# A causal convolution followed by a routed mixture of experts: band built through DRAM, weights issued earlier, routing steps, outputs and the last slot placed anew

## The chip, the cores and the metric

The kernel runs on one core of one Trainium2 chip. The core has a matrix engine (TensorE, PE in the profile; its weight loads are shown as PEld), a vector engine (VectorE, DVE), a scalar engine (ScalarE, ACT), GpSimd (POOL) and a queue engine for transfers (SyncE, SP). Each engine works through its own instructions in order. Transfers are issued by SP, ScalarE or POOL and are moved by 16 DMA engines.

The metric is the device time of one execution in microseconds; lower is better. Times of several executions are given by their median. The profile is of one execution, whose own time stands beside it.

## What is computed

The reference, cut to what matters: x has shape (8, 3584, 192), there are 8 heads of 24 channels with 7 taps each, and 8 experts of width 1024.

```python
w = np.exp(weight - weight.max(-1, keepdims=True))
w = w / (w.sum(-1, keepdims=True) + 1e-09)               # softmax over 7 taps
out = np.einsum('hk,bskhg->bshg', w, x_unf)              # causal window of 7 rows
x = out.reshape(28672, 192)

logits = x @ w_gate                                      # 192 x 8
e_idx = np.argmax(logits, axis=1)
gate_w = probs[np.arange(N), e_idx]                      # softmax of the logits
eom = 1.0 / (1.0 + np.exp(-(x @ w_output_gate)))
for e in range(8):
    mask = e_idx == e
    h = np.maximum(x[mask] @ w1[e], 0.0)                 # 192 -> 1024
    out[mask] = gate_w[mask, None] * eom[mask, e, None] * (h @ w2[e])
```

## The kernel before

**Units.** The 28672 tokens are worked in 16 units of 1792 tokens, each of 16 blocks of 112. A unit passes three stages: front_a (convolution and router logits), front_b (routing: sorting its rows by expert into a stream in DRAM), and slots (the experts on 512 rows of one expert each).

**The constants ahead.** The taps (cw, L108) are loaded by SP, then the input of units 0 and 1 (load_x, L85 to L100, three transfers each for the first unit of a sequence, two otherwise). The taps' softmax is made by VectorE and ScalarE (L123 to L133). The convolution is a matmul against a band matrix per head, 118 input rows by 112 output rows. The band is filled by 14 predicated copies on VectorE (L142), each of which writes one tap of four heads along a diagonal, with a mask cut from an identity matrix (idp, L137). The router's weights wg come by eight small transfers on ScalarE's queue (L128, L129). The experts' weights stay resident in wres; they come in 32 pieces, four per expert, through POOL's queue. load_w(n) (L218) issues the next n of them.

**front_a(u)** (L298) is a generator with 16 steps. Eight steps are the convolution's matmuls, one head each (L303), with a copy out of PSUM into cv. Six steps are groups of four transposes (L317) with a copy into tt. One step is the router's matmul (L326) with the copy lt (L331), and the last is four transposes back (L335) and VectorE's copy gb (L340). After the convolution the input of unit u + 2 is requested (L309).

**evac** (L284) does the copies out of PSUM. It alternates between ScalarE and VectorE by the bit sync_flip, unless evac_on names an engine; while `fill` is not None, which is so ahead of the rounds, all go to ScalarE. In the rounds the front's PSUM tiles (pf) take turns in two banks.

**front_b(u)** (L347) has 12 steps. Step 1: the maximum, mask and exponent (L351 to L367, VectorE). Step 2: counts per expert (L374 on TensorE; nu, np, og and the gate gs on VectorE, L377 to L393). Step 3: prefix sums (L396 to L399 on TensorE, dm and pos on VectorE). Step 4: the first permutation masks and the destinations dd, dst, du (L431 to L446). Steps 5 to 12: for each pair of blocks four permutation matmuls (L457), a copy xs, and a scatter into the stream in DRAM (L475), which POOL issues from a list of pending ones (emit_in).

**Rounds.** After units 0, 1 and 2 have gone through both stages (L697 to L711), rounds follow for u = 2 to 15 (L742). A round has four slots (the last one eight full and three half ones, which bring their own copy of an expert's weights), and a slot has four positions, so a round has 16. At each position stand, in an order written out by hand: half of a slot's first layer at even positions (Slot.first, L626 and L633; ReLU on ScalarE, L646, for three quarters and on VectorE, L644, for the last), a quarter of the second layer of the slot before (second, L668), its copy y (L674) and output (L495, an indirect transfer issued by POOL, 128 rows each), steps of front_a(u + 2), steps of front_b(u + 1) (named fs) and of front_b(u + 2) (named fbn). The slots' input is read at position 7 for the round after (loads, L720).

Engines run in order, so the place of a step in this list is the place of its work on each engine. POOL's list holds scatters, outputs and weight issues. The transfers of SP and ScalarE share eight landing counters in the order of issue, and POOL has eight more; an issue waits until the transfer before it on its counter has landed.

Of the kernel before, what the change touches and what calls it, by code (L numbers as in the profile page):

```python
# [21 lines left out]
def kernel(  # L22
# [10 lines left out]
    nc = tc.nc  # L33
# [51 lines left out]
    def load_x(u):  # L85
# [8 lines left out]
        if u % UPB == 0:  # L94
# [14 lines left out]
                                    ap=[[0, 128], [KW, H], [1, KW]]))  # L109
    xts = {0: load_x(0)}  # L110
    xts[1] = load_x(1)


    ones_t = const.tile([128, 128], FP32)
    nc.vector.memset(ones_t, 1.0)
    identf = const.tile([128, 128], FP32)
    nc.gpsimd.affine_select(out=identf, in_=ones_t, pattern=[[-1, 128]],
                            compare_op=ALU.is_equal, fill=0.0, base=0,
                            channel_multiplier=1)
    band = const.tile([128, H, BT], FP32)  # L120
    nc.vector.memset(band, 0.0)
    cmx = const.tile([128, H], FP32)
# [3 lines left out]
    nc.scalar.activation(out=cw, in_=cw, func=AF.Exp)  # L126
    for i, (p0, p1, d0) in enumerate([(0, 128, 0), (0, 64, 128), (64, 128, 0), (0, 128, 64)]):
        nc.scalar.dma_start(wg[p0:p1, i, 0:E], moe_w_gate[d0:d0 + p1 - p0, :])  # L128
        nc.scalar.dma_start(wg[p0:p1, i, E:2 * E], moe_w_output_gate[d0:d0 + p1 - p0, :])  # L129
    csm = const.tile([128, H], FP32)  # L130
# [3 lines left out]
                            op=ALU.mult)  # L134

    idp = ps_f.tile([128, 512], FP32, tag="pf", name="idp")
    nc.vector.tensor_copy(out=idp[:, 0:128], in_=identf)  # L137
    idpu = idp.bitcast(U32)
    for h in (0, H // 2):
        for k in range(KW):  # L140
            m = idpu[:, k:k + BT]
            nc.vector.copy_predicated(  # L142
                out=band[:, h:h + H // 2, :],
                mask=m.unsqueeze(1).to_broadcast([128, H // 2, BT]),
                data=cw[:, h:h + H // 2, k:k + 1].to_broadcast([128, H // 2, BT]))
    ltri = const.tile([128, 128], FP16)
# [25 lines left out]
    idu = const.tile([128, NB], U32)  # L172
    nc.gpsimd.iota(idu, pattern=[[-BT, NB]], base=NOID, channel_multiplier=-1)
    idl = const.tile([128, NB], U32)
# [21 lines left out]
    nc.vector.tensor_copy(out=pos16, in_=poi.rearrange("p r j -> p (r j)"))  # L196

    wres = const.tile([128, E * WE], FP16)

    def w_pieces(e):
        o = e * WE
        w = moe_w1[e]
        return [
            (wres[:, o:o + F].rearrange("p (l c) -> p l c", l=2),
             bass.AP(tensor=w.tensor, offset=w.offset,
                     ap=[[F, 128], [64 * F + F // 2, 2], [1, F // 2]])),  # L210
            (wres[0:64, o + F:o + WA], w[0:64, F // 2:F]),
            (wres[64:128, o + F:o + WA], w[128:D, 0:F // 2]),
            (wres[:, o + WA:o + WE].rearrange("p (c d) -> p c d", d=D),
             moe_w2[e].rearrange("(c p) d -> p c d", p=128))]

    wq = deque(p for e in range(E) for p in w_pieces(e))

    def load_w(n):  # L218

        while n and wq:  # L220
            nc.gpsimd.dma_start(*wq.popleft())
            n -= 1

# [27 lines left out]
    for l in range(2):  # L251
# [7 lines left out]
        in0=o9, in1=s9, op=ALU.subtract)  # L259
    nc.vector.tensor_copy(out=lsum[:, c0 + 2 * NSEG:NK], in_=eqe[:, 0:E])  # L260


# [35 lines left out]
    def front_a(u, ahead=True):  # L298
# [31 lines left out]
        lt = pct.tile([128, 4 * BT], FP32, tag="lt", name="lt")  # L330
        evac(lt, pl[:, 0:4 * BT])  # L331
        yield
# [157 lines left out]

    def emit_out():

        while pout:
            y, oi, j = pout.popleft()
            i = nc.gpsimd.indirect_dma_start(  # L495
                out=out, out_offset=bass.IndirectOffsetOnAxis(ap=oi[:, j:j + 1], axis=0),
                in_=y[:, j, :], in_offset=None, bounds_check=N - 1, oob_is_err=False)
            nodep(i, "out", ("out",))
            last[0] = "out"
# [108 lines left out]
    class Slot:  # L608
        def __init__(self, xabi, w, inv):
            self.xa, self.xb, self.xi = xabi  # L610
            self.w, self.inv = w, inv
            self.n = self.xa.shape[1]
            self.nq = self.n // 128
            self.ht = []
# [34 lines left out]
        def second(self, q):  # L649
            if q >= self.nq:  # L650
                return
            if q == 0:
# [9 lines left out]
                                        op=ALU.bitwise_or)  # L662
            if q % 2 == 0:
                self.pp = ps_y.tile([128, 512], FP32, tag="py", name="pyt")
            o = (q % 2) * D
            for fc in range(FCH):
                w = WA + (fc // 2 + fc % 2 * (FCH // 2)) * D
                nc.tensor.matmul(self.pp[:, o:o + D],  # L668
                                 self.ht[fc // 2][:, fc % 2, q * 128:(q + 1) * 128],
                                 self.w[:, w:w + D],  # L670
                                 start=(fc == 0 and q % 2 == 0),
                                 stop=(fc == FCH - 1 and q % 2 == 1))
            if q % 2 == 1:
                nc.scalar.copy(out=self.y[:, q - 1:q + 1, :],  # L674
# [21 lines left out]

    load_w(8)  # L697
    drain(front_a(0))

    for u in range(U0 + 1):  # L700
# [3 lines left out]
        while drain(fb, 1):  # L704
            n += 1

            drain(fa, 1 if u == U0 or n > 8 else 2 if n < 8 else 0)
            emit_in(len(pend))
            if u < U0 and n > 4 and n % 2:
                load_w(1)  # L710
# [24 lines left out]
    fbn = front_b(U0 + 1)  # L735
    drain(fbn, 4)
    fill[0] = None

    prev = None
    for u in range(U0, NU):  # L742
        fs, fa, fbn = fbn, iter(()), iter(())
        if u + 2 < NU:
            fa, fbn = front_a(u + 2), front_b(u + 2)
        k = 0
        while k < len(todo):
            w, inv, xabi = todo[k]
            s = Slot(xabi, w, inv)
            for q in range(4):  # L750
                pos = 4 * k + q
                if 0 <= 16 * (u - U0) + pos - 4 < 16:
                    load_w(1)
                if q % 2 == 0:
                    s.first(q // 2)
                if pos in (0, 2, 4, 6, 8, 10, 12):
                    evac_on[0] = "act" if pos < 8 else None
                    drain(fa, 1)
                if pos == 14:
                    drain(fbn, 1)  # L760
                if prev is not None:
                    prev.second(q)
                    emit_out()
                if pos in (1, 3, 5, 7, 8, 9, 10, 11):
                    evac_on[0] = "dve" if pos < 8 else None
                    drain(fa, 2 if pos == 9 else 1)
                if pos < 8:
                    evac_on[0] = "act"
                    drain(fs, 1)
                    evac_on[0] = None  # L770
                    emit_in(len(pend))
                if pos == 12:
                    drain(fbn, 1)
                if pos == 15:
                    drain(fbn, 2)
                if pos == 7 and u + 1 < NU:
                    nxt = loads(u + 1)
# [65 lines left out]
```

## Time and profile before

| what | value |
|---|---|
| median of 9 runs | 624.03 us (622.06 to 626.73) |
| the profiled execution | 622.7 us |
| its span | 621.0 us |
| mean granted TensorE clock | 0.987 |
| first convolution starts | 11.17 us |
| first slot starts | 79.56 us |
| last output issued in the rounds | 613.11 us |
| POOL: outputs (L495) | 246, 996 ns each |
| POOL: scatters (L475) | 128, 1036 ns each |
| ScalarE: ReLU (L646) | 189, 1002 ns each |
| mean DMA rate | 142 GB/s, 88.12 MB |

In the profile a row of the timeline has the start in us, the duration in us, the engine, the line, the operation, the tiles (out<-in), and a count; in brackets is how long the engine had been idle before, and what ended that. A row of the groups has the busy time and the mean of one in ns, then the idle time before it with what ended most of it. The PEclk row gives the granted clock in tenths over 40 slices of the span. A row of the windows has the length, then for each engine the busy time and the number of instructions (PE, PEld, DVE, ACT, POOL), the granted clock, the share of the DMA engines and the GB/s.

### The profile page before, as it was taken

How to read it: one execution, taken by the hardware profiler on the slowest of the kernel's cores; microseconds unless marked ns; L12 is line 12 of the kernel's file. 1: busy time of each engine (PE TensorE's matmuls, PEld its weight loads, DVE VectorE, ACT ScalarE, POOL GpSimd, SP SyncE). 2: the span in 40 equal slices, each digit the busy share in tenths (PEclk: the TensorE clock that was granted, in tenths of full speed). 3: DMA queues.
4: the chain of work that ended last, by engine and by line, in shares of the span. 5: the costliest groups of instructions: out<-in, count | busy, mean ns of one | idle time of the engine just before them, and what ended most of it. 6: DMA issues, size and time to landing. Idle time of an engine off the chain costs nothing.

```text
span 621.0 us, 13578 instructions
## 1 busy us (share of the span) xinstructions
PE 574.3 (92%) x4544; PEld 358.5 (58%) x4544; DVE 380.8 (61%) x1310; ACT 382.4 (62%) x638; POOL 403.1 (65%) x419
## 2 busy tenths in 40 slices
PE   2999689999999999999999999999999999989992
PEld 1565337565566656656665666656566575646562
DVE  7678664765839477484856749476683947626231
ACT  1677556665666756665675666667566665657761
POOL 1377537787775757667575766757676675776674
PEclk9999979999999999999999999999999999999998
DMA  5999758993845455373555637255473425256631
GB/s 151 202 205 250 185 103 197 159 253 106 178 136 123 161 125 165 101 192 99 111 161 113 179 101 184 90 115 161 109 195 91 105 80 115 83 116 141 186 106 42
DMA packets 162567, 88.12 MB, mean 142 GB/s; under 512 B 116765, under 2 KB 153792, under 8 KB 162496
## 3 DMA queue, kind: packets, MB, share of 16 engines
q1 hardware_dynamic: 131872, 43.92, 31.5%
q0 software_dynamic: 29728, 43.30, 26.5%
q8 instruction: 36, 0.59, 0.4%
q14 instruction: 35, 0.29, 0.2%
q10 hardware_dynamic: 896, 0.03, 0.1%
HBM read 35.92 MB, written 43.06 MB: 127 GB/s over the span
## 4 chain that ended last, share of the span: by engine, by line
PE 78%; DVE 8%; ACT 5%; DMA 4%; issue 2%; POOL 1%; SPq 0%; ACTq 0%; POOLq 0%; DVEq 0%
PE pyt L668 21%; PE pp L626 18%; PE pf L303 11%; PE pp L633 10%; PE pf L457 7%; PE pf L317 5%; PE pf L326 4%; ACT ht L646 3%; DVE ht L644 2%; DVE band L142 1%; DMA xb<-xcg_sorted 1%; PE pf L335 1%; DMA out_dram<-y,oi 1%; ACT cv L291 1%; DMA xcg_sorted<-xs,du 1%
## 5 line engine op out<-in xcount | busy, mean ns | idle before, releaser
L495 POOL DMA_INDIRECT out_dram<-y,oi x246 | 244.9, 996 | 120.0 <-ACT y L674 54.4
L646 ACT ACTIVATE ht<-pp 128x1024 f16<-128x1024 f32 (+1 forms) x189 | 182.9, 1002 | 57.6 <-PE pp L633 56.7
L668 PE MATMUL pyt<-wres,ht 128*128 128x192 f16 x1920 | 190.4, 246 | 0.0
L475 POOL DMA_INDIRECT xcg_sorted<-xs,du x128 | 132.6, 1036 | 74.0 <-ACT xs L291 32.5
L668 PEld LDWEIGHTS <-ht 128*128 128x128 f16 x1968 | 166.5, 97 | 23.9 <-issue 10.4
L644 DVE TENSOR_SCALAR ht<-pp 128x1024 f16<-128x1024 f32 (+1 forms) x63 | 75.4, 1198 | 72.1 <-PE pp L626 72.1
L303 PE MATMUL pf<-xt,band 118*112 118x384 f32 x256 | 105.1, 504 | 11.7 <-DMA wg<-n_moe_w_output_gate_dram 11.2
L626 PE MATMUL pp<-xa,wres 128*128 128x512 f16 x240 | 93.0, 388 | 5.8 <-DMA xa<-xcg_sorted 5.8
L626 PE MATMUL pp<-xb,wres 128*128 128x512 f16 x240 | 91.3, 380 | 1.7 <-DMA xb<-xcg_sorted 1.7
L291 ACT CAST xs<-pf 128x388 f16<-128x388 f32 x128 | 61.8, 486 | 50.1 <-PE pf L457 48.4
L674 ACT COPY y<-pyt 128x384 f32<-128x384 f32 x123 | 58.5, 476 | 35.1 <-PE pyt L668 31.1
L626 PEld LDWEIGHTS <-wres 128*128 128x128 f16 x480 | 33.8, 97 | 67.7 <-issue 62.8
L633 PE MATMUL pp<-xa,wres 64*128 64x512 f16 x240 | 72.8, 383 | 0.0
L633 PE MATMUL pp<-xb,wres 64*128 64x512 f16 x240 | 72.8, 383 | 0.0
L457 PE MATMUL pf<-xrow,pm 112*128 112x194 f16 x512 | 64.5, 247 | 7.8 <-ACT cv L291 4.0
L457 PEld LDWEIGHTS <-pm 112*128 112x128 f16 x512 | 45.1, 98 | 35.1 <-issue 12.5
L427 DVE TENSOR_SCALAR pm<-pos,pos 112x256 f16<-112x256 f16 x256 | 62.8, 310 | 0.0
L422 DVE TENSOR_TENSOR xrow<-cv,gs 112x384 f16<-112x384 f32 x121 | 62.0, 551 | 0.0
L303 PEld LDWEIGHTS pf<-xt,band 118*112 118x112 f32 x256 | 41.5, 182 | 27.2 <-DVE band L142 12.1
L293 DVE COPY cv<-pf 112x384 f32<-112x384 f32 x48 | 26.5, 552 | 43.4 <-PE pf L303 43.3
L291 ACT COPY cv<-pf 112x384 f32<-112x384 f32 x80 | 38.1, 479 | 21.6 <-PE pf L303 21.2
L317 PE MATMUL pf<-identf,cv 112*128 112x112 f32 x384 | 49.3, 259 | 0.7 <-ACT cv L291 0.7
(135 smaller groups left out, 432.7 us busy)
## 6 DMA issues: line engine op xcount, KB each, us to landing
xt<-in_x_dram SPq DMA_DIRECT2D x8, 1344.0 KB
xt<-in_x_dram SPq DMA_DIRECT2D x8, 1260.0 KB
out_dram<-y,oi POOLq DMA_INDIRECT x246
wres<-in_moe_w_dram POOLq DMA_DIRECT2D x8, 384.0 KB
wd<-wres SPq DMA_DIRECT2D x3, 768.0 KB
wres<-in_moe_w_dram POOLq DMA_DIRECT2D x8, 256.0 KB
xcg_sorted<-xs,du POOLq DMA_INDIRECT x128
xcg_sorted<-zrow SPq DMA_DIRECT2D x8, 256.0 KB
```

The source lines that it names most:

```text
L291: nc.scalar.copy(out=o, in_=i)
L303: nc.tensor.matmul(pc[0:BT, 0:NB * GH], band[0:KI, h, :], xt[0:KI, :, h * GH:(h + 1) * GH], start=True, stop=True)
L317: nc.tensor.matmul(pt[:, j * BT:(j + 1) * BT], cvf[0:BT, m * 2 * D + i * 128:m * 2 * D + (i + 1) * 128], identf[0:BT, 0:BT], is_transpose= ...
L427: nc.vector.tensor_scalar(out=pms[i][P, l, :], in0=pos16[P], scalar1=pos[P, l * NG + i:l * NG + i + 1], scalar2=None, op0=ALU.is_equal)
L457: nc.tensor.matmul(ps[:, r * XW:(r + 1) * XW], pm[P, l, r * 128:(r + 1) * 128], xr[P, l * NG + i, :], start=(r == 0 and l == 0), stop=(r = ...
L475: i = nc.gpsimd.indirect_dma_start(out=xcg2, out_offset=bass.IndirectOffsetOnAxis(ap=du[:, i:i + 1], axis=0), in_=xs.rearrange("p r w -> p ...
L495: i = nc.gpsimd.indirect_dma_start(out=out, out_offset=bass.IndirectOffsetOnAxis(ap=oi[:, j:j + 1], axis=0), in_=y[:, j, :], in_offset=Non ...
L626: nc.tensor.matmul(pps[r][:, l, :], w[:, o2:o2 + 128], x, start=(r == 0), stop=(r == 1))
L633: nc.tensor.matmul(pps[r][:, l, :], w[p0:p0 + 64, c:c + 128], x[p0:p0 + 64], start=(r == 1), stop=(r == 0))
L644: nc.vector.tensor_relu(out=ht, in_=pps[r])
L646: nc.scalar.activation(out=ht, in_=pps[r], func=AF.Relu)
L668: nc.tensor.matmul(self.pp[:, o:o + D], self.ht[fc // 2][:, fc % 2, q * 128:(q + 1) * 128], self.w[:, w:w + D], start=(fc == 0 and q % 2 = ...
```

## The change

- **wg** comes on SP's queue, between the inputs of units 0 and 1, instead of on ScalarE's.
- **The band.** Only heads 0 and 1 are filled by predicated copies (seven of 2 x 112). For heads 2 to 7 ScalarE copies the taps into a row of zeros, one line of 229 per head; the lines go to DRAM, and a second transfer reads the band from them, each partition one element further along. This gives the rows of a block in reverse order, so the mask comes from an anti-diagonal matrix (antif), and the row numbers (idu) count the other way.
- **Weights.** Twelve pieces are issued right after the constants, ahead of zrow and front_a(0), instead of eight after them; four more in the opening's loop for unit 0 alone, instead of four each for units 0 and 1. The other sixteen go at positions 8 to 23 of the rounds instead of 4 to 19.
- **front_a(0).** The copies of its six transposes alternate between ScalarE and VectorE; ahead of the rounds the copy lt is split in two halves, one per engine.
- **First round.** One step of unit 3's front_b is done ahead of the first slot instead of four; the others stand in the round, at positions 0 to 10, with two at position 2.
- **Order in a round.** Steps of front_a ahead of the second layer stand at positions 0, 2, 4, 6, 8, 9, 10 instead of 0, 2, ..., 12; those of fbn at 12, 13 (after it) and 14, 15 (before it) instead of 12 (after), 14 (before) and two at 15 (after).
- **Round 14** keeps up to eight outputs in the list during its first eight positions.
- **The last slot** has its own PSUM tile, copy and output for each 128 rows.

```diff
@@ -108,41 +108,56 @@
     xts = {0: load_x(0)}
+    for i, (p0, p1, d0) in enumerate([(0, 128, 0), (0, 64, 128), (64, 128, 0), (0, 128, 64)]):
+        nc.sync.dma_start(wg[p0:p1, i, 0:E], moe_w_gate[d0:d0 + p1 - p0, :])
+        nc.sync.dma_start(wg[p0:p1, i, E:2 * E], moe_w_output_gate[d0:d0 + p1 - p0, :])
     xts[1] = load_x(1)
...
+    antif = const.tile([128, 128], FP32)
+    nc.gpsimd.affine_select(out=antif, in_=ones_t, pattern=[[1, 128]],
+                            compare_op=ALU.is_equal, fill=0.0, base=-127,
+                            channel_multiplier=1)
...
+    HB = 2
+    LW = BT + KI - 1
     band = const.tile([128, H, BT], FP32)
-    nc.vector.memset(band, 0.0)
+    nc.vector.memset(band[:, 0:HB, :], 0.0)
+    wline = const.tile([1, H - HB, LW], FP32)
+    nc.vector.memset(wline, 0.0)
+    wldr = nc.dram_tensor("tap_lines", (H - HB, LW), FP32, kind="Internal").ap()
...
-    for i, (p0, p1, d0) in enumerate([(0, 128, 0), (0, 64, 128), (64, 128, 0), (0, 128, 64)]):
-        nc.scalar.dma_start(wg[p0:p1, i, 0:E], moe_w_gate[d0:d0 + p1 - p0, :])
-        nc.scalar.dma_start(wg[p0:p1, i, E:2 * E], moe_w_output_gate[d0:d0 + p1 - p0, :])
...
+    nc.scalar.copy(out=wline[:, :, BT - 1:KI], in_=cw[0:1, HB:H, :])
+    nc.scalar.dma_start(wldr, wline)
+    nc.scalar.dma_start(band[0:KI, HB:H, :],
+                        bass.AP(tensor=wldr.tensor, offset=wldr.offset,
+                                ap=[[1, KI], [LW, H - HB], [1, BT]]))
     idp = ps_f.tile([128, 512], FP32, tag="pf", name="idp")
-    nc.vector.tensor_copy(out=idp[:, 0:128], in_=identf)
+    nc.vector.tensor_copy(out=idp[:, 0:128], in_=antif)
     idpu = idp.bitcast(U32)
-    for h in (0, H // 2):
-        for k in range(KW):
-            m = idpu[:, k:k + BT]
...
+    for k in range(KW):
+        m = idpu[:, 128 - BT - k:128 - k]
+        nc.vector.copy_predicated(
+            out=band[:, 0:HB, :],
+            mask=m.unsqueeze(1).to_broadcast([128, HB, BT]),
+            data=cw[:, 0:HB, k:k + 1].to_broadcast([128, HB, BT]))
...
-    nc.gpsimd.iota(idu, pattern=[[-BT, NB]], base=NOID, channel_multiplier=-1)
+    nc.gpsimd.iota(idu, pattern=[[-BT, NB]], base=NOID - (BT - 1), channel_multiplier=1)
...
+    load_w(12)
...
-        evac(lt, pl[:, 0:4 * BT])
+        if fill[0] is None:
+            evac(lt, pl[:, 0:4 * BT])
+        else:
+            nc.scalar.copy(out=lt[:, 0:2 * BT], in_=pl[:, 0:2 * BT])
+            nc.vector.tensor_copy(out=lt[:, 2 * BT:4 * BT], in_=pl[:, 2 * BT:4 * BT])
...
-    def emit_out():
-        while pout:
+    def emit_out(keep=0):
+        while len(pout) > keep:
...
-            if q % 2 == 0:
+            if q % 2 == 0 or self.end:
                 self.pp = ps_y.tile([128, 512], FP32, tag="py", name="pyt")
...
-            if q % 2 == 1:
+            if self.end:
+                nc.scalar.copy(out=self.y[:, q, :], in_=self.pp[:, 0:D])
+                pout.append((self.y, self.oi, q))
+            elif q % 2 == 1:
...
-    load_w(8)
-    drain(front_a(0))
+    fa = front_a(0)
+    drain(fa, H)
+    for i in range(6):
+        evac_on[0] = "dve" if i % 2 else "act"
+        drain(fa, 1)
+    evac_on[0] = None
+    drain(fa)
...
-            if u < U0 and n > 4 and n % 2:
+            if u == 0 and n > 4 and n % 2:
                 load_w(1)
...
     fbn = front_b(U0 + 1)
-    drain(fbn, 4)
+    drain(fbn, 1)
     fill[0] = None
...
+        last_s = 10 if u == U0 else 7
...
-                if 0 <= 16 * (u - U0) + pos - 4 < 16:
+                if 0 <= 16 * (u - U0) + pos - 8 < 16:
                     load_w(1)
                 if q % 2 == 0:
                     s.first(q // 2)
-                if pos in (0, 2, 4, 6, 8, 10, 12):
-                    evac_on[0] = "act" if pos < 8 else None
+                evac_on[0] = "act" if pos < 8 else None
+                if pos in (0, 2, 4, 6, 8, 9, 10):
                     drain(fa, 1)
-                if pos == 14:
+                if u == U0 and pos == 2:
+                    drain(fs, 1)
+                if pos in (14, 15):
                     drain(fbn, 1)
                 if prev is not None:
                     prev.second(q)
-                    emit_out()
+                    emit_out(8 if u == NU - 2 and pos < 8 else 0)
+                evac_on[0] = "dve" if pos < 8 else None
                 if pos in (1, 3, 5, 7, 8, 9, 10, 11):
-                    evac_on[0] = "dve" if pos < 8 else None
                     drain(fa, 2 if pos == 9 else 1)
-                if pos < 8:
+                if pos <= last_s and not (u == U0 and pos == 2):
                     evac_on[0] = "act"
                     drain(fs, 1)
-                    evac_on[0] = None
                     emit_in(len(pend))
-                if pos == 12:
+                evac_on[0] = None
+                if pos in (12, 13):
                     drain(fbn, 1)
-                if pos == 15:
-                    drain(fbn, 2)
-                if pos == 7 and u + 1 < NU:
+                if pos == last_s and u + 1 < NU:
                     nxt = loads(u + 1)
```

## The prediction

> **What bounds the kernel now.** I read the page's engine rows first, then its groups, then the timeline of three stretches: the opening, a round in the middle, the end.
>
> ```profile
> PE 574.3 (92%) x4544; PEld 358.5 (58%) x4544; DVE 380.8 (61%) x1310; ACT 382.4 (62%) x638; POOL 403.1 (65%) x419
> PEclk9999979999999999999999999999999999999998
> ...
> L457 PE MATMUL pf<-xrow,pm 112*128 112x194 f16 x512 | 64.5, 247 | 7.8 <-ACT cv L291 4.0
> ```
>
> TensorE is busy for 92% of the span, so in the middle only its waits can be won. From round 3 to round 13 a round's first matmul follows the last one's by 36.67 us (timeline), and each round holds two waits over 0.12 us:
>
> ```profile
> 482.46 1.23 DVE L644 TENSOR_SCALAR ht<-pp 128x1024 f16<-128x1024 f32 x1 [0.44 <-PE pp L626]
> ...
> 484.40 0.23 PE L398 MATMUL pf<-lsum,np 64*128 64x128 f16 x1 [0.31 <-DVE og L384]
> ```
>
> L398 needs np, which VectorE makes only after this 1.23 us ReLU. The second is L457's, 0.40 us in that round: ScalarE empties the conv's PSUM bank late. The opening has other limits:
>
> ```profile
> 0.82 3.76 DMA cw<-in_weight_dram
> ...
> 11.17 4.37 PE L303 MATMUL pf<-xt,band 118*112 118x384 f32 x8 [11.17 <-DMA wg<-n_moe_w_output_gate_dram]
> 15.87 2.83 PE L303 MATMUL pf<-xt,band 118*112 118x384 f32 x8 [0.33 <-DVE band L142]
> ...
> 24.61 2.10 PE L303 MATMUL pf<-xt,band 118*112 118x384 f32 x6
> ...
> 72.73 0.98 POOL L475 DMA_INDIRECT xcg_sorted<-xs,du  x1 [1.90 <-DMA xcg_sorted<-xs,du]
> 74.02 0.98 POOL L475 DMA_INDIRECT xcg_sorted<-xs,du  x1 [0.30 <-DVE dl L353]
> ...
> 79.56 0.59 PE L626 MATMUL pp<-xa,wres 128*128 128x512 f16 x1 [3.44 <-DMA xa<-xcg_sorted]
> ```
>
> conv(0) waits for x(0) (11 us; the releaser named is a neighbour on the same counters) and half way for the band. conv(1) starts at 24.61 when unit 0's last transposes leave TensorE. The first slot starts at 79.56, behind the last scatter at 74.02. The end belongs to POOL:
>
> ```profile
> 545.50 0.98 POOL L475 DMA_INDIRECT xcg_sorted<-xs,du  x1 [0.30 <-ACT ht L646]
> ...
> 575.78 0.98 POOL L495 DMA_INDIRECT out_dram<-y,oi  x1 [3.55 <-ACT y L674]
> ...
> 613.11 0.99 POOL L495 DMA_INDIRECT out_dram<-y,oi  x1 [0.30 <-DMA out_dram<-y,oi]
> ```
>
> From 575.78 on POOL issues an output every 1.287 us without a gap.
>
> **The change, part by part.** The sum goes against the profiled 622.7 (span 621.0 and 1.7 around it); the median, 624.03, is 1.33 above that, which I add at the end.
>
> *1. Band and conv(0): 0.* Fourteen copies of 448 (9.49 us for x14) become seven of half the width; by half the duration 7 x 0.33 = 2.3 us, so VectorE runs 7.1 us ahead, and heads 0 and 1 are ready at 8.7, before x(0). Heads 2 to 7 go tap copy, DMA to DRAM, DMA back. The only row for a small load's whole way is cw, 3.76: 6.4 + 3.76 + 3.76 = 13.9, with issue about 14.4. The slower row is wg's (issued 5.53, landed 11.12: 5.6 us), which gives 17.6. I take 14.4, as cw moves on an empty queue as this does, though x(0) is in flight beside it. Then conv(0) ends at 18.3 instead of 18.55 (bounds -0.7 and +1.8), and with the two copy engines and the halved lt copy gb is ready some 0.4 earlier. That gain is lost in the next term.
>
> The Trainium skill ("DMA: Bandwidth & Descriptors", section "Anatomy of one DMA") gives a fixed cost of about 2.0 us for one DMA, and this trace shows 3.76 for 28 KB. By the page the band would be there at 10.4 and x(0) alone would set conv(0); by the row it is four us later. The row decides, and the sum would be 0 by either.
>
> *2. Unit 1's input: +3.4.* The load of x(1), issued at 11.14 before, now stands on SP behind the eight wg loads. SP and ScalarE share the landing counters in their order of issue, so wg's last load waits for the band's landing; x(1) is issued at about 14.6. Beside it POOL now issues twelve weight pieces as soon as VectorE has made eqe (18.52 - 7.1 = 11.4): data from about 15.2 (first issue 19.07 to first data 3.2 us in the trace). x(1) is 1.45 MB. Alone, at the 206 GB/s that the windows show for 11 to 18 us, it lands at 14.6 + 1 + 7.0 = 22.6 and nothing is late. With weights beside it:
>
> ```profile
> 22.00:33.00 11.00, 9.91 (x58) 5.65 (x52) 7.33 (x30) 6.36 (x17) 2.70 (x5) 1.00 1.29 228
> ```
>
> Half of 228 GB/s is 12.7 us: x(1) at 28.4, conv(1) 3.8 later. There the software and the hardware queue did move equal shares (1.46 and 1.45 MB in 18 to 33), so I take the half. 0.4 of it was won before: +3.4. Bounds: 0, and +7.4 if the band lands at 17.6 (x(1) issued 18.5, landed 32.3).
>
> *3. POOL before the first slot: -3.1.* Four weight issues in unit 1's phase go. The last xs of unit 2 is ready at 69.2, yet the last scatter is issued at 74.02, since scatters queue 1.29 us apart behind weights and 1.90 us for a counter. By xs alone it would be 70.9: -3.1. Bounds 0 and -4. First slot: 79.56 + 3.4 - 3.1, about 79.9. Only one step instead of four of unit 3 stands ahead of it: 0, TensorE waits there anyway; the cover is the 3.44 us of the row, and without it the steps would cost 3 us.
>
> *4. The clock at the first slot: 0.*
>
> ```profile
> 79.50:90.00 10.50, 9.78 (x36) 3.97 (x37) 5.12 (x19) 5.38 (x8) 1.96 (x2) 0.69 0.50 97
> ```
>
> 0.69 granted is half clock for 62% of 10.5 us, a loss of 3.25. The wait ahead of it shrinks from 7 to about 4 us and loses its few matmuls. It may keep the clock (-3.25) or not (0); a new wait of 4 us for x(1) may itself cost up to 3.25. Nearest is the row itself, so 0.
>
> The Trainium skill ("TensorE: Matmul & The Clock Gate", section "What's actually happening") says that an idle window of about 3.4 us halves the clock and a busy one of that length restores it. That speaks against the change, since part 2 makes a second wait above that length. By the rule the sum would be up to 3.3 higher than by the row.
>
> *5. Steps of unit 3 moved into the first round: +0.45.* L374 and L396 to L399 now stand between slots; beside the wait they took 482.36 to 482.51 and about 0.30 more.
>
> *6. Rounds: -3.4.* The counts step moves two positions forward and the prefix step one. L374 then comes 1.52 us before L396, with no ReLU in front of nu and np (0.9 us): L398's wait goes (3.5 of its 4.1 us lie in rounds). The moved prefix also leaves L457 the bank that is not ScalarE's: it then needs dd 2.63 us after the group, TensorE arrives after 2.83, so its wait goes too (4.0 and 0.40 for dd): -7.9. In their place: the transposes of group 2 directly follow group 1. A round has 23 alternating copies, so in every other round ScalarE has group 0's copy, behind
>
> ```profile
> 468.79 1.94 ACT L646 ACTIVATE ht<-pp 128x1024 f16<-128x1024 f32 x2 [0.34 <-PE pp L633]
> ...
> 470.61 0.54 ACT L291 COPY tt<-pf 128x448 f32<-128x448 f32 x1
> ```
>
> and ends at 471.15, where the bank is wanted at 470.66: 0.49. L335 then follows the lt copy with 0.09 (ScalarE) or 0.18 us (VectorE) missing: 0.75 per two rounds, six times, +4.5. Net -3.4; bounds -7.9 (VectorE takes the copies) and 0 (the waits only change place). Two points make the net fragile: the 0.2 us of slack at L457, and which engine the alternation hits. Weights later in the rounds (positions 8 to 23): 0, covered by some 9 us before a slot of that expert; without cover a piece late by one position costs 2.3 us.
>
> *7. The end: -0.6.* Outputs held back let the last scatter of round 14 go at 537.9 instead of 545.50, which removes waits of 2.04 and 0.66 us at 551. But POOL then has 58 outputs from 539.1 on: the last at 539.1 + 57 x 1.287 = 612.5, against 613.11. The 3.55 us gap is all that it can close, and most of that is taken by the outputs held. The split last slot: 0, as its y is ready 2.3 us before POOL gets to it. If POOL had the room, 2.7 could come.
>
> Sum: 0 + 3.4 - 3.1 + 0 + 0.45 - 3.4 - 0.6 = -3.25. 622.7 - 3.25 + 1.33 = 620.8. Own range 618.5 to 623.
>
> **The rivals.** *B, the opening gains too, 616.5.* x(1) in time (-3.4: 617.4) or the clock kept at the first slot (617.5), both 614.1. For it: x(1) lands at 22.6 if the hardware queue keeps its 206 GB/s. Against: the equal shares.
> *C, slower, 628.* x(1), queued behind the chain of tap line and band, lands at 32.3 (+4.0 over my term) and TensorE, idle for 8 us, returns at half clock (+3.25): 620.8 + 7.25. It is slower than before from a start of conv(1) at about 30.3 with the clock closed, 33.5 without. For it: 5.6 us of the wg row; against: cw's 3.76.
> *D, the waits in the rounds change place only, 624.2* (620.8 + 3.4). For it: ScalarE's queue at 468.79 stands before group 0's copy in any round; against: L398's cause, the ReLU, is really gone.
>
> **How the numbers follow.** A 0.42, B 0.22, C 0.20, D 0.16. A measurement of this kernel tells about 0.3% (1.9 us) from no change: faster is below 622.2, slower above 625.9. Faster: 0.33 of A, all of B, 0.02 of D: 0.57. Slower: 0.17 of C, 0.04 of D: 0.21. The rest, 0.22, is the same. The range 614 to 627 takes in B down to both gains and C up to a start of conv(1) near 31; about 0.15 is left out.
>
> **What would show it.** In the new profile: conv(1) at 28.4 with a wait for x(1) over 3 us (C: past 30.3; B: under 25). The last scatter before the first slot within 2 us of the last xs. L398 with waits under 0.1 in the rounds and none on cv at L457; new waits at L317 in every other round of about 0.5 and L335 of 0.1 to 0.2; first-to-first about 36.4. No wait at 551 for xa, POOL without a gap from there, and the last output issued within 1 us of 612.5 - 2.6. I am wrong if conv(1) keeps its start, if a round gains over 0.6 us or loses, or if POOL has gaps after 550.

## The result, and the profile after

The change makes the kernel slower: 647.29 us (median of 10 runs, 645.03 to 649.6) against 623.84 us before (31 runs), a ratio of 1.0375 with a 95% interval of 1.0354 to 1.0397. The forecast was 620.8 with a range to 627, so sign and range were wrong. The profiled execution has a span of 644.1 us against 621.0.

The starts of the slots' first matmuls (L626 before, L647 after) part the 23.1 us by stage:

| stage | before, us | after, us | difference |
|---|---|---|---|
| start to first slot | 79.56 | 102.23 | +22.67 |
| round u = 2 | 37.35 | 43.06 | +5.71 |
| rounds 3 and 4 | 74.34 | 74.67 | +0.33 |
| rounds 5 to 13 | 330.06 | 325.55 | -4.51 |
| round 14 | 29.90 | 26.81 | -3.09 |
| round 15 to the end | 69.79 | 71.78 | +1.99 |

So nearly all of it is lost ahead of the first slot, and a quarter of that again in the first round; the later rounds do gain. The page of the changed kernel, engine rows and slices first, then a DMA queue, then two groups:

```profile
PE 578.0 (90%) x4544; PEld 358.8 (56%) x4544; DVE 379.0 (59%) x1312; ACT 378.6 (59%) x635; POOL 408.4 (63%) x420
...
PE   1079986989999999999999999999999999999991
...
q10 hardware_dynamic: 712, 0.32, 0.2%
...
L320 PE MATMUL pf<-xt,band 118*112 118x384 f32 x256 | 106.4, 510 | 33.4 <-DMA band<-tap_lines 21.3
...
L478 PE MATMUL pf<-xrow,pm 112*128 112x194 f16 x512 | 64.7, 247 | 5.9 <-DVE pm L448 4.4
```

TensorE's second slice is empty (a slice is 16 us), and the convolution's idle time is now the band's transfer, 21.3 us, which was not there before. q10 carries the tap lines and the band: 712 packets for 0.32 MB. L478 (L457 before) no longer waits for cv.

The chain of what ended last, in the opening (start, duration, what):

```profile
0.82 3.52 DMA cw<-in_weight_dram
...
6.13 5.97 DMA tap_lines<-wline
...
12.13 23.31 DMA band<-tap_lines
...
35.48 4.76 PE pf L320 x8
```

The taps go out in 5.97 us and come back as a band in 23.31. The timeline of SP shows what else hangs on that landing:

```profile
12.63 0.58 SPq L112 DMA_DIRECT2D wg<-in_moe_w_gate_dram  x1
35.46 0.33 SPq L113 DMA_DIRECT2D wg<-n_moe_w_output_gate_dram  x1
35.84 0.43 SPq L98 DMA_DIRECT2D xt<-in_x_dram  x1
```

wg's last load shares the band's landing counter and stands until 35.46, with unit 1's input behind it. conv(1) starts at 47.30, 22.69 later than before, which is the whole delay of the first slot.

The end of the first round, from TensorE's timeline:

```profile
145.29 0.59 PE L647 MATMUL pp<-xa,wres 128*128 128x512 f16 x1 [3.06 <-DMA xa<-xcg_sorted]
146.09 0.58 PE L647 MATMUL pp<-xb,wres 128*128 128x512 f16 x1 [0.22 <-DMA xb<-xcg_sorted]
```

TensorE waits for the second round's slots, which had no such wait before. The waits of TensorE between 182 and 545 us (total, times, longest):

```profile
PE pf L334 <- ACT tt L308: 1.7, 5, 0.3
```

The two waits of each round before, for og and for cv, are gone; in every other round there is the transposes' wait.

### The profile page after: what moved, and what is told of

It is laid out like the page before. It is cut to its first block, busy times and chain, and to the rows that moved or that the text cites. A ratio compares the mean times of both kernels' runs of the same rounds, so it can differ in the third digit from the quotient of the medians.

```text
span 644.1 us, 13571 instructions
## 1 busy us (share of the span) xinstructions
PE 578.0 (90%) x4544; PEld 358.8 (56%) x4544; DVE 379.0 (59%) x1312; ACT 378.6 (59%) x635; POOL 408.4 (63%) x420
## 3 DMA queue, kind: packets, MB, share of 16 engines
HBM read 36.24 MB, written 43.06 MB: 123 GB/s over the span
## 4 chain that ended last, share of the span: by engine, by line
PE 79%; DMA 10%; DVE 4%; ACT 3%; issue 2%; POOL 1%; SPq 0%; POOLq 0%; ACTq 0%; DVEq 0%
PE pyt L689 23%; PE pp L647 17%; PE pf L320 12%; PE pp L654 10%; PE pf L478 6%; PE pf L334 5%; PE pf L343 4%; DMA band<-tap_lines 4%; DMA xb<-xcg_sorted 2%; ACT ht L667 2%; DMA out_dram<-y,oi 2%; PE pf L356 1%; DMA xcg_sorted<-xs,du 1%; DMA tap_lines<-wline 1%; POOL out_dram L516 1%
## 5 line engine op out<-in xcount | busy, mean ns | idle before, releaser
L516 POOL DMA_INDIRECT out_dram<-y,oi x246 | 248.1, 1009 | 114.7 <-ACT y L698 47.7
L496 POOL DMA_INDIRECT xcg_sorted<-xs,du x128 | 135.0, 1054 | 100.2 <-ACT xs L308 67.9
L320 PE MATMUL pf<-xt,band 118*112 118x384 f32 x256 | 106.4, 510 | 33.4 <-DMA band<-tap_lines 21.3
L647 PE MATMUL pp<-xa,wres 128*128 128x512 f16 x240 | 93.3, 389 | 8.2 <-DMA xa<-xcg_sorted 7.9
L647 PE MATMUL pp<-xb,wres 128*128 128x512 f16 x240 | 91.8, 382 | 1.1 <-DMA xb<-xcg_sorted 1.1
L320 PEld LDWEIGHTS pf<-xt,band 118*112 118x112 f32 x256 | 42.2, 185 | 50.4 <-DMA band<-tap_lines 22.4
L478 PE MATMUL pf<-xrow,pm 112*128 112x194 f16 x512 | 64.7, 247 | 5.9 <-DVE pm L448 4.4
L647 PEld LDWEIGHTS <-wres 128*128 128x128 f16 x480 | 34.8, 98 | 60.7 <-issue 60.3
L448 DVE TENSOR_SCALAR pm<-pos,pos 112x256 f16<-112x256 f16 x256 | 64.6, 321 | 0.0
L478 PEld LDWEIGHTS <-pm 112*128 112x128 f16 x512 | 44.4, 97 | 30.9 <-issue 13.7
```

The costliest lines, as they stand in the source:

```text
L320: nc.tensor.matmul(pc[0:BT, 0:NB * GH], band[0:KI, h, :], xt[0:KI, :, h * GH:(h + 1) * GH], start=True, stop=True)
L448: nc.vector.tensor_scalar(out=pms[i][P, l, :], in0=pos16[P], scalar1=pos[P, l * NG + i:l * NG + i + 1], scalar2=None, op0=ALU.is_equal)
L478: nc.tensor.matmul(ps[:, r * XW:(r + 1) * XW], pm[P, l, r * 128:(r + 1) * 128], xr[P, l * NG + i, :], start=(r == 0 and l == 0), stop=(r = ...
L496: i = nc.gpsimd.indirect_dma_start(out=xcg2, out_offset=bass.IndirectOffsetOnAxis(ap=du[:, i:i + 1], axis=0), in_=xs.rearrange("p r w -> p ...
L516: i = nc.gpsimd.indirect_dma_start(out=out, out_offset=bass.IndirectOffsetOnAxis(ap=oi[:, j:j + 1], axis=0), in_=y[:, j, :], in_offset=Non ...
L647: nc.tensor.matmul(pps[r][:, l, :], w[:, o2:o2 + 128], x, start=(r == 0), stop=(r == 1))
```

## The experiments

Each kernel was compared with runs of the kernel before on the same chip, so the ratios are what to compare. In the expectations the rounds are counted from the first as 0: "rounds 3 to 11" are u = 5 to 13. The start of conv(1) in the changed kernel that the first one gives as 49.8 is that of a later group; it is 47.30.

### Why the band's read takes 23 us

**Two transfers for the band, 112 and 6 rows.**

```diff
-    nc.scalar.dma_start(band[0:KI, HB:H, :], ...)
+    for r0, r1 in ((0, BT), (BT, KI)):
+        nc.scalar.dma_start(band[r0:r1, HB:H, :], ...offset + r0...)
```

> The changed kernel, but the band's read from the tap lines is two transfers, rows 0 to 111 and rows 112 to 117, instead of one of 118 rows. Three theories of why the read took 23.3 us (issued 12.13, landed 35.48). S (spread): a transfer of 118 rows falls on few of the 16 DMA engines; early in it, 95 packets of 34 ns came per us, the work of about 3 engines. Then the band lands before 18 us, conv(1) starts near 30 instead of 49.8, and the time falls by 17 to 20 to 627 to 630. W (weights): the twelve early weight pieces crowd out any read beside them. Then the split changes nothing: landing after 30, time 645 to 649. N (narrow rows): reading 448-byte rows one element apart is slow however it is cut. Then the landing is after 30 as well, time 645 to 649.

Measured: 636.65 us, ratio 1.0180 (1.0127 to 1.0232). The band is there at 15.6 us, with 397 packets in the fullest microsecond instead of 95. S, that the read is spread over few engines, is right about the landing. The time fell by about 11 us and not by 17 to 20, for two reasons that TensorE's timeline shows:

```profile
11.58 2.87 PE L321 MATMUL pf<-xt,band 118*112 118x384 f32 x4 [11.58 <-DVE pe L225]
15.90 7.23 PE L321 MATMUL pf<-xt,band 118*112 118x384 f32 x12 [1.45 <-DMA band<-tap_lines]
...
34.16 4.15 PE L321 MATMUL pf<-xt,band 118*112 118x384 f32 x6 [5.10 <-DMA xt<-in_x_dram]
```

After the pause of 1.45 us the twelve matmuls take 0.60 us each; in the kernel before the second eight took 0.35 each. conv(0) ends at 23.0 instead of 18.6. And conv(1) waits 5.10 us for its input and then takes 4.15 us for six matmuls instead of 2.10. The window of these six has the reason (the three figures at its end are the granted clock, the share of 16 DMA engines, and GB/s):

```profile
34.10:38.30 4.20, 4.14 (x7) 1.74 (x8) 0.00 (x0) 1.17 (x3) 0.00 (x0) 0.50 1.16 262
```

TensorE comes out of this wait at half clock.

**The weights held until the band has landed.** GpSimd first copies one element of the band's last head.

```diff
+    bseen = const.tile([1, 1], FP32)
+    nc.gpsimd.tensor_copy(out=bseen, in_=band[0:1, H - 1, 0:1])
     load_w(12)
```

> The changed kernel, but GpSimd first reads one element of the band from DRAM, so that the twelve weight pieces are issued after the band's landing. The read has the DMA engines almost to itself. S: 708 packets at the 95 per us seen early in it take 7.5 us, landing at 20.5 to 22, time about 634 to 637. W: landing before 17, time about 627 to 630. N: like S or later.

Measured: 637.43 us, ratio 1.0213 (1.0174 to 1.0252); the second part of conv(0) starts at 22.47 after 8.12 us of waiting. The landing (22.4) and the time lie just beyond what S named, and far from W's: without the weights the read is still slow, 10 us from its issue, and with them it takes 23. So both count. The window in which nothing but the band moves:

```profile
15.00:20.00 5.00, 0.00 (x0) 0.00 (x0) 0.00 (x0) 0.00 (x0) 0.00 (x0) 1.00 0.15 40
```

0.15 of 16 engines is 2.4. Where all are at work the same figure is about 1.1 per engine (1.09 between 16 and 17 us before, as x loads), so about two of sixteen move the band.

**One transfer of 128 rows.** The lines are ten zeros longer, and ten more rows are read that nothing uses.

```diff
-    LW = BT + KI - 1
+    LW = BT + 127
-    nc.scalar.dma_start(band[0:KI, HB:H, :], ... [[1, KI], ...
+    nc.scalar.dma_start(band[0:128, HB:H, :], ... [[1, 128], ...
```

> The changed kernel with the band read in one transfer, of 128 rows instead of 118 (the lines in DRAM ten zeros longer, ten more rows that nothing reads). It parts two readings of the split's gain. Row count: a count that 16 divides (128, like 112) spreads over all DMA engines; then one transfer lands as early as the split did, 15 to 17, more than 250 packets in its fullest us, time 634 to 639. Rival, number of transfers: each transfer gets few engines, and two got more than one; then the landing stays after 28 and the time at 645 to 649.

Measured: 636.98 us, ratio 1.0226 (1.0196 to 1.0255). The band lands in time for 16.00, as with the split, and 415 packets come in the fullest microsecond. Its window:

```profile
14.00:15.00 1.00, 0.55 (x1) 0.00 (x0) 0.00 (x0) 0.41 (x1) 1.00 (x3) 1.00 0.94 190
```

0.94 instead of 0.15, and some 185 of the 190 KB in this window are the band's (415 packets, nearly all of 448 bytes). The packets also count the engines: beside the band's 708 packets of 448 bytes the trace of the changed kernel has 2 packets of 4 bytes at the end of the read, that of the split 22, and that of this run, beside 768, 16. One closing packet for each engine that takes part would be 2, 16 + 6 and 16. It is the count of rows, not of transfers.

**Unit 1's input ahead of wg,** in the kernel with the split.

```diff
     xts = {0: load_x(0)}
+    xts[1] = load_x(1)
     for i, (p0, p1, d0) in enumerate(...):      # wg
...
-    xts[1] = load_x(1)
```

> The run with the split read of the band (e1_split), with the input of unit 1 issued on SP ahead of the eight wg loads again. In e1 conv(1) waited 5.1 us for it and its first six matmuls then took 4.15 us instead of 2.10. Theory (x(1) is late because it stands behind wg's last loads, which wait for the band's landing, and then shares the DMA engines with the weights): the wait goes, conv(1) starts within 1 us after unit 0's last transposes, the first slot comes 5 to 8 us earlier (84 to 87), time 629 to 632. Rival: x(1) then runs beside x(0) and the tap line and makes the band land later; first slot after 89, time above 634.

Measured: 637.09 us, ratio 1.0201 (1.0169 to 1.0234), the first slot at 90.80 instead of 91.51. The rival is right. conv(1) follows at once (35.79 after transposes from 35.09), so the wait was indeed that of the order on SP. But the tap line and the band then move beside x(1): the band's last part comes at 23.1 instead of 15.6, and the delay has only changed its place.

In all four of these runs the first slot starts between 90.80 and 91.55 and conv(1) between 33.90 and 35.79, though the band is there at 15.6, 16.0, 22.4 or 23.1. So the two engines and the weights beside them make about half of the 22.7 us. The other 11 us stay as long as the band, wg and x(1) hang on one another and x(1) or the band shares the DMA engines with other loads; these two causes were not parted.

### The rest of the change without the band

**VectorE's band in the changed kernel.** Fourteen predicated copies again, with the reversed mask; no tap lines.

> The changed kernel with the whole band made by VectorE again (14 predicated copies of four heads), no tap lines; all other parts as changed. If the read of the band is the cause of the 22.67 us by which the first slot came later (102.23 against 79.56), the first slot is back at 77 to 81 and the time at 621 to 626: the rounds' gain of 4.5 in rounds 3 to 11 against a first round that is 5.7 longer. If the twelve early weight pieces, wg on SP's queue or the missing routing steps are the cause, the first slot stays above 85 and the time above 630.

Measured: 626.46 us, ratio 1.0032 (1.0002 to 1.0061), half a microsecond above what was expected; the first slot is at 80.39. Without the band's transfer 21.8 of the 22.7 us are gone. One more thing changes with it: GpSimd's weights wait for eqe, which VectorE now makes behind the fourteen copies, and are issued from 19.82 instead of 12.39. That this is not the cause is shown by the run with the weights held: there they are issued from 22.61, and the first slot is at 91.55. But the first round takes 45.14 us and the second 39.40, which the rounds' gain does not pay. TensorE's row at the second round's first slot, and the window of that slot:

```profile
125.53 0.59 PE L638 MATMUL pp<-xa,wres 128*128 128x512 f16 x1 [2.81 <-DMA xa<-xcg_sorted]
```

```profile
125.50:138.60 13.10, 12.58 (x72) 7.35 (x73) 6.68 (x26) 6.43 (x10) 8.76 (x10) 0.75 1.17 195
```

A wait of 2.81 us, and after it a granted clock of 0.75 over 13.1 us, which at half clock for half of that time is another 3.3 us.

**Four routing steps ahead again,** in the kernel just shown.

```diff
-    drain(fbn, 1)
+    drain(fbn, 4)
...
-        last_s = 10 if u == U0 else 7
+        last_s = 7
...
-                if u == U0 and pos == 2:
-                    drain(fs, 1)
```

> The run with VectorE's band (e3_oldband), with four routing steps of unit 3 ahead of the first slot again instead of one, and so the next round's slots read at position 7 of the first round instead of 10. In e3 the first round took 45.1 us and the second 39.4 against 37.35 and 36.93 before: PE waited 2.8 us for xa at 125.5 and then ran at half clock for half a slot. Theory: this is the price of the missing steps (late scatters, late reads, and the clock that falls with the wait); the first round goes back to 37 to 38, the second to about 36.2, the first slot stays within 1.5 us of 80.4, and the time is 616 to 619. Rival: it is the weights at positions 8 to 23 that hold the scatters up on GpSimd; then the first round stays above 41 and the time above 621.

Measured: 619.23 us, ratio 0.9922 (0.9893 to 0.9950), just above the 616 to 619 expected. The first round is 37.09 and the first slot at 80.41, both as the theory has them. The second round is 37.64 instead of about 36.2, and u = 4 took 39.16, with weights still being issued. The window of the same slot as above now has the full clock:

```profile
117.50:127.10 9.60, 9.60 (x74) 6.10 (x73) 9.09 (x34) 6.69 (x11) 8.07 (x10) 1.00 1.35 201
```

The wait that the theory names is not the largest part of the missing 8 us. The four slots of the first round, each from its first matmul to the next slot's:

| kernel | slot 1, us | slot 2 | slot 3 | slot 4 |
|---|---|---|---|---|
| before | 10.91 | 9.62 | 9.71 | 7.11 |
| changed | 11.73 | 9.62 | 12.16 | 9.55 |
| VectorE's band, one step ahead | 14.06 | 9.62 | 12.16 | 9.31 |
| VectorE's band, four steps ahead | 10.26 | 9.62 | 10.88 | 6.33 |

The wait for the next slots is in the last column (3.0 us more), the moved steps stand in the third (1.3 us more). The first column (3.8) shows what the three steps did ahead of the slot: without them TensorE idles 4.7 us in one piece there, with them 2.1 and 1.5, and the granted clock of the first 11 us, with one step and with four, is 0.51 and 0.80:

```profile
80.40:91.40 11.00, 10.06 (x28) 3.04 (x28) 3.23 (x13) 3.76 (x5) 0.00 (x0) 0.51 0.43 78
```

```profile
80.40:91.40 11.00, 10.11 (x44) 4.07 (x46) 8.11 (x31) 6.03 (x10) 2.99 (x3) 0.80 0.49 98
```

In the six kernels of this study with one step ahead the first slot took 11.73 to 14.06 us, in the eight with four 10.26 to 11.57.

**The rounds alone.** The kernel before up to the first slot, the changed kernel's order in the rounds and its end.

> The kernel before up to the first slot (its band, wg, weights, four routing steps ahead, weights at positions 4 to 19), with the changed order in the rounds, the outputs held in round 14 and the split last slot. Rounds 3 to 11 gained 0.50 us each in the changed kernel; if that holds for all twelve, and the end gives 0.4, the time is 623.8 - 6.4, 617 to 618, and the first round is no longer than 37.4. Rival: the gain came with the rounds' phase against the weights and the first round's cost of 5.7 is part of the new order; then 620 to 624.

Measured: 617.50 us, ratio 0.9902 (0.9868 to 0.9936), as expected. The first round takes 37.23; later rounds take 35.94 and 36.45 in turn, against 36.67. TensorE's waits from 190 to 480 us, of the kernel before and of this one:

```profile
PE pf L457 <- ACT cv L291: 3.2, 8, 0.4
PE pf L398 <- DVE og L384: 2.6, 8, 0.3
```

```profile
PE pf L317 <- ACT tt L291: 1.3, 4, 0.3
```

Two waits in each of eight rounds against one in each of four.

**The front's steps at the old positions,** the routing steps at the new ones.

```diff
-                if pos in (0, 2, 4, 6, 8, 9, 10):
+                if pos in (0, 2, 4, 6, 8, 10, 12):
```

> The rounds-only kernel (e4_rounds) with the first front's steps at the old positions 0, 2, 4, 6, 8, 10, 12, and the routing steps at the new ones. It parts the rounds' gain of 0.71 us from the new wait. Theory: the gain is that of the routing steps (L398 and L457 no longer wait), and the transposes of group 2 directly behind group 1 cost 0.33 in every other round; the old positions take that away, so that rounds go from 35.95 on average to 35.75 to 35.85 and the time falls by 1 to 2. Rival: with the old positions the mask is made just before L374, which then waits for VectorE, 0.3 to 2 us in each round; time longer by 3 or more.

Measured: 624.78 us, ratio 1.0005 (0.9990 to 1.0021). The theory fell, the rival is right. The rounds take 36.97, and TensorE waits (190 to 480 us):

```profile
PE pf L374 <- DVE msk L367: 8.1, 7, 1.2
```

The wait for the transposes is gone, and one of 1.2 us for the mask stands in each round. The front's steps have to be earlier for the routing steps to be earlier; the 0.3 us in every other round is the price of that.

### Term 3 and the end

**Four outputs held, and none held, in round 14** (in the rounds-only kernel, `emit_out(4 ...)` and `emit_out()`).

> The rounds-only kernel with four outputs held in round 14 instead of eight. Theory: four outputs of 1.287 us go into the 3.3 us of gaps, and the last scatter, 1.3 to 2.6 us later, still lands ahead of its readers; the last output comes 88 to 89.5 us after the round's first slot instead of 91.4, time 614 to 615.5. Rival: the outputs delay the scatters and TensorE waits at the last round's first slot; no gain, 617 to 618.

> The rounds-only kernel (e4_rounds) with no outputs held back in round 14. Theory (the end belongs to GpSimd): holding trades a wait of TensorE at the first slot of the last round (2.7 us before) for gaps on GpSimd in round 14 (3.3 us beyond its usual 0.3), so without it the last output is issued 90 to 92.5 us after the round's first slot, as with it (91.4), time 616 to 619. Rival (the end belongs to TensorE): the wait comes back in full and the time is 2 to 3 us longer, about 620.

Measured with four: 616.12 us, ratio 0.9872 (0.9849 to 0.9896), the last output 90.74 us after the round's first slot (609.98 - 519.24). Against 91.41 with eight that is 0.7 of the 1.9 to 3.4 expected, and the intervals of the two ratios overlap. Measured with none: 620.60 us, ratio 0.9935 (0.9908 to 0.9962), the last output 94.30 after the first slot. This was the rival's time. TensorE's wait from 517 us on, and the window behind it:

```profile
PE pp L626 <- DMA xa<-xcg_sorted: 3.2, 1, 3.2
```

```profile
547.10:555.90 8.80, 8.42 (x49) 4.79 (x50) 1.15 (x2) 3.55 (x4) 5.65 (x7) 0.66 0.71 131
```

A wait of 3.2 us, then a clock of 0.66 over 8.8 us, which costs TensorE 3.0 more. With the outputs ahead of them the scatters come later, and so do the reads of the last round: the last scatter is issued 24.11 us after the round's first slot, with four held 21.29, with eight 16.74. Round 14 is 3.35 us longer than with eight (30.16 against 26.81), which is the wait; the lower clock behind it does not reach the end, where GpSimd's outputs run on. Holding outputs is worth 2.9 us in the new order.

**The last slot by 256 rows again.**

> The rounds-only kernel with the last slot's copies and outputs by 256 rows again. Theory: its y is ready before GpSimd gets to it, so nothing changes: last output within 0.5 us of 91.4 after the first slot of round 14, time within 1 us of e4's. Rival: the split lets the last output start earlier; then 1 to 2 us longer.

Measured: 617.74 us, ratio 0.9908 (0.9874 to 0.9943); the last output 91.33 after the first slot, 0.08 from that with the split. The split end is worth nothing here, as expected.

**Twelve weight pieces early, none in unit 1's phase,** in the kernel with four outputs held.

```diff
-    load_w(8)
+    load_w(12)
...
-            if u < U0 and n > 4 and n % 2:
+            if u == 0 and n > 4 and n % 2:
```

> The rounds-only kernel with four outputs held (e7_keep4), with twelve weight pieces ahead of the first convolution and four in unit 0's loop, so that none is issued in unit 1's phase. This is the prediction's term 3 alone: if the scatters before the first slot are late because of weight issues between them, the last one comes about 3 us earlier (73.5 to 70.5), the first slot is at 75 to 77 and the time 612.5 to 614.5. Rival: the scatters follow the copies xs, and GpSimd only hides behind them; first slot within 1 us of 78.8, time 615 to 617.5.

Measured: 615.39 us, ratio 0.9877 (0.9833 to 0.9920). The last scatter ahead of the first slot goes at 71.59 instead of 73.51 with four outputs held (73.16 with eight), and the first slot starts at 77.17 instead of 78.87. That lies between the theory and the rival, half of the 3 us; the time is in the rival's range. No weight stands between the last scatters any more, but they still follow one another about 1.3 us apart on GpSimd. This kernel and the one with four outputs held are the fastest of the study, 1.2 to 1.3% faster than the kernel before; which of the two is faster can't be told from these runs.

## Why the prediction was wrong, point by point

1. **Band and conv(0), "0", landing at 13.9 to 17.6: this is the step that failed.** The term was put at nothing. I priced both transfers by the taps' load (3.76) and bounded them by wg's (5.6). The tap line took 5.97, just outside the bounds, beside x(0) (7.39 in the run where x(1) was on its way as well), and the band's read 23.31. The load that I took for the price has 128 rows, the band 118. The runs show what the count does: 118 rows go over two DMA engines (a share of 0.15 alone, 10 us from the issue), 128 rows over sixteen (landing 3.5 us after the issue, and 3.4 for 112 + 6). With the early weights on the same engines the 10 us become 23. TensorE waited 21.27 us for the band where I had counted almost none, and the first slot came 22.7 us later. Half of that goes away with the two engines; the rest is what hangs on the transfer (point 2). The kernel itself held the hint: load_x takes its 118 rows in pieces of 112 and 6.

   The Trainium skill states this in "DMA: Bandwidth & Descriptors", section "Why a DMA increments its semaphore by 16 and not by 1": a transfer uses the largest number of engines, up to 16, that divides the slowest dimension on both sides. For 118 that is 2, which agrees with the 2.4 / 1.1 engines measured and with the two closing packets. I had weighed another sentence of that page, the fixed 2.0 us, against the trace, and this one not at all; and that figure is fitted there to transfers issued by GpSimd, while cw, the tap line and the band go through the queues of SP and ScalarE.

2. **Unit 1's input, "+3.4".** In the changed kernel it did not show: it is issued at 35.84 and conv(1) follows unit 0 without a wait, since unit 0 is later still. With the band's read repaired it shows as I had worked it out, only larger: a wait of 5.10 instead of 3.8, conv(1) at 34.16 where I had 28.4. x(1)'s large part was issued at 17.26, 2.7 us later than I had it, and took 16.8 us beside the weights where I had 13.7. The queue behind wg's last load was right, and it was the mechanism of rival C, whose landing of the band (17.6 at the latest) was 18 us short.

3. **GpSimd before the first slot, "-3.1".** Mis-sized: alone it gives 1.6 to 1.9 us at the last scatter and 1.7 at the first slot, as the scatters are 1.3 us apart without weights too. In the changed kernel it gave nothing: from conv(1) to the last scatter are 49.40 us, and were 49.41. The last xs ends 46.59 us after conv(1) there, 44.62 before; what in the new opening delays it by 2 us was not tried. The "0" for the three steps that no longer stand ahead of the slot was wrong (point 5).

4. **The clock at the first slot, "0".** Right in the changed kernel: 0.77 over 102.2 to 113.9 against 0.71 over 79.5 to 90.5. The second wait that I had weighed, for x(1), came only with the band's read repaired, and the clock fell with it (0.50 behind 5.10 us). What I missed is that it also falls at the second round's first slot (0.85 over 11.3 us in the changed kernel, 0.75 over 13.1 with VectorE's band).

5. **Steps moved into the first round, "+0.45".** This failed too: 5.7 us in the changed kernel, and 7.8 and 2.5 in rounds 2 and 3 with VectorE's band (45.14 and 39.40 against 37.35 and 36.93 before). I counted the steps' matmuls on TensorE and not what moves with them: the last scatters are three positions later, the reads of the next round's slots go from position 7 to 10, and the slot that needs them waits, then runs at half clock. In part 3 I had called the cover ahead of the first slot free. It was for the start of the slot (80.39 with one step, 80.41 with four), but not for its clock: with nothing to do in the wait TensorE ran that slot at 0.51 instead of 0.80, and it took 14.06 us instead of 10.26.

6. **Rounds, "-3.4".** Right in its mechanism, low in size. The gain is 0.73 us in a round without the new wait (36.67 to 35.94), which is the 0.31 and 0.40 of the two waits, and the new wait costs 0.50 in every other round where I had 0.75. The run with old positions shows that both belong together. In the changed kernel rounds 5 to 13 gained 4.51 us.

7. **The end, "-0.6".** The last output came 91.42 us after round 14's first slot instead of 91.80: -0.4. POOL had no gap from 562.26 on, and the split end was worth nothing, as said. That in the new order the clock falls at the last round without the held outputs (0.66 over 8.8 us) I had not seen.

Without points 1, 2 and 5 the sum would have been right in sign: the rounds alone, with the end, are 6.0 us faster than the kernel before.

## What to carry to other kernels

Before a transfer is priced by a row of the trace, compare the number of rows, not only the bytes: a count with no large divisor up to 16 (here 118: two engines, against sixteen for 128) puts the whole transfer on few DMA engines, and it is then at the mercy of whatever else these move. When a step is moved later, follow what it feeds up to the next engine that reads it; here the larger price was not the step but the read behind it, and the wait that the step had filled. A wait of about 3 us on TensorE can cost more than its length, since the clock fell behind it: by 3.3 us more after 2.81, by 1.7 after 3.06, by 3.0 after 3.2. After the 2.04 us ahead of the last round in the kernel before it stayed at 1.00.

## What the runs showed of the hardware that was not expected

- The granted clock of the views says nothing about the first microseconds. The convolution's first matmuls start 0.64 us apart in every kernel and 0.32 us apart later, and the windows show 1.00 for both. The change of pace falls on the trace's first clock record: at 14.30 us in the kernel before, 22.20 in the split run, 39.41 in the changed kernel; a stretch with no record counts as 1.00. Where there is a record, behind the wait for x(1) in the split run, the 0.64 us go with a clock of 0.50. So the first matmuls most likely run at half clock too, but no record shows it directly. By that reading the twelve matmuls of the split run took 0.60 us each because they began, behind a pause of 1.45 us, 6.3 us before the full pace came. What sets that moment was not tried.
- Between rounds of the same form single waits for xa of up to 3 us appear while the last weights are being issued: round u = 3 to the first slot of u = 4 ends with a step of 6.61, 7.37, 8.00 or 9.29 us in four kernels that do not differ up to there. In the last of them the clock fell as well (0.85 over the next 11.6 us). That is a spread of about 3 us in one execution, and it stays open what sets it. From u = 5 on the same kernels agree within 0.02 us in every round up to 13.
